# A fused attention and feed-forward kernel: the two weights of an f loaded by one transfer and converted together in operations of 128x768

## The chip, the cores and the metric

One core of a Trainium2 chip. The metric is the device time in microseconds from the start to the end of the kernel. TensorE (PE in the profile, its weight loads PEld) multiplies matrices; the vector engine (DVE) and the scalar engine (ACT) work elementwise; GpSimd (POOL) has only a few fills here; SyncE (SP) issues most of the DMAs, some are issued by ACT.

## The reference

```python
def _attn_ref(q, k, v, beta):                       # each [4, 8, 768, 48], beta [4, 8, 768]
    k_n = k / (np.linalg.norm(k, axis=-1, keepdims=True) + 1e-06)
    for t in range(S):
        kt, vt, bt = (k_n[:, :, t], v[:, :, t], beta[:, :, t, None])
        y[:, :, t] = np.einsum('bhd,bhde->bhe', q[:, :, t], state)
        v_old = np.einsum('bhde,bhd->bhe', state, kt)
        state = state + bt[:, :, :, None] * np.einsum('bhd,bhe->bhde', kt, vt - v_old)
    return y

def _moe_ref(x, w_in, w_out):                       # x [3072, 384], w_in [384, 2048], w_out [2048, 384]
    h = x @ w_in
    g = np.maximum(0.01 * h, h)
    return g @ w_out
```

The output of the first, with its heads laid side by side, is the x of the second.

## The kernel before, in words

The sequence is cut into 12 blocks of 64 steps (`nblk`); a block holds these steps of all four sequences, 256 tokens. Five streams of work run over the blocks. `gram(n)` multiplies keys and queries of a block with its keys (tiles `kq`, `pg`, copied to `gs`) and sends the products through DRAM (`gd`) into the matrix `L`. `inv(b)` inverts the triangular matrix of a block on the vector engine, in 31 elimination steps of short operations on tiles `tmp` and `T` (L263, L268); blocks 0 and 1 are inverted together in the first round, each later block in a round of its own, which begins with a memset of `T` (L280). `solve(n)` carries the recurrent state through the block on TensorE and leaves y in `ys`. `columns(n)` transposes y into x (`px`) and splits it into a high and a low half, `xh` and `xl` (L116). `ffn(n)` is the second part of the reference: for each of 16 pieces f of the hidden width (128 columns each) nine matrix products into `ph` (L468), the activation on ACT (`gh`), the low half `gl` on DVE (L475), and six products into `po` (L458), which follow two f later. At its end two copies `ob` and four output transfers.

All matrix products of the feed-forward part work on pairs of a high and a low part. The weights come from DRAM as 64-bit words, two 32-bit words for each weight (`wr`, 128x384 weights of w_in or of w_out for an f, 384 KB), and `weights()` makes both parts of them once, in block 0. For a piece k (f = k // 2; even k is w_in, odd k w_out) it is: Abs on ACT (L146), a clamp (L148, TENSOR_SCALAR), shift and mask (L154, TENSOR_SCALAR), sign (L155, SCALAR_TENSOR_TENSOR) on `cg`; the rest of the mantissa `cr` (L156, TENSOR_SCALAR, and L157, SCALAR_TENSOR_TENSOR); the exponent `ce` (L158, TENSOR_SCALAR); the cast of `cg` to the high part of `w` on ACT (L160); the low part of `w` on DVE (L161, SCALAR_TENSOR_TENSOR). Raw words and finished weights share a place in memory: the high part is written over the raw words, so the cast waits for L157, which reads them last. There are three `cg` buffers, one `cr` and one `ce`.

What sets the order: the main loop's `weave` calls the streams in turn, in block 0 the conversion over the first 12 of 17 slots; `behind(name)` tells the scheduler not to place an instruction ahead of a marked one. From that a scheduler of the framework fixes the order on each engine. Four pieces (`KA`) are converted ahead of the first inverse, 14 (`WEARLY`) are loaded early, and each later one is loaded eight pieces ahead (`WAHEAD`): the transfer of piece k + 8 waits for a small memset of its tile (L123), which is placed behind the clamp of piece k. Transfers of the weights are issued on SP.

Of the kernel before, what the change touches and what calls it, by code (L numbers as in the profile page):

```python
# [9 lines left out]
F32 = mybir.dt.float32  # L10
F32R = mybir.dt.float32r
U32 = mybir.dt.uint32
U64 = mybir.dt.uint64
AF = mybir.ActivationFunctionType
ALU = mybir.AluOpType
# [16 lines left out]
P = 128  # L32
# [15 lines left out]
def delta_moe_kernel(ctx: ExitStack, tc, kqT, kv, qT, beta, cst, w_all, out, nblk):  # L48
# [10 lines left out]
    nc = tc.nc  # L59
    NFC, _, DO = w_all.shape[1:]  # L60
    NCC = DO // P
    NTB = TB // P

    st = ctx.enter_context(tc.tile_pool(name="st", bufs=1))
    sb = ctx.enter_context(tc.tile_pool(name="sb", bufs=2))
# [34 lines left out]
    def identities():  # L100
        for t in ring["k"]:
            nc.vector.tensor_copy(
                t[0:R0].rearrange("p h u t -> p (h u) t"),
                eye[0:R0, 0:D].rearrange("p (o t) -> p o t", o=1).broadcast_to([R0, GH, D]))


    wi, wo = ([{}, {}] for _ in range(2))
    raws, mark = {}, {}

    def behind(name):  # L110

        return tc.issue_after(mark[name]) if name in mark else nullcontext()
# [2 lines left out]
        nc.scalar.copy(hi, src)  # L115
        nc.vector.tensor_tensor(lo, src, hi.bitcast(F32), ALU.subtract)  # L116

    def load_w(k, gate=None):
        if k < 2 * NFC:
            raws[k] = raw = sb.tile([P, DO], U64, tag=f"w{k}", name=f"wr{k}", bufs=1)  # L120
            if gate:
                with behind(gate):
                    nc.vector.memset(raw[:, 0:1].bitcast(F32), 0.0)  # L123
            with behind("L"):
                nc.sync.dma_start(raw, w_all[:, k // 2, k % 2])

    def weights():

        for k in range(2 * NFC):
            f, x = k // 2, k % 2
            words = raws.pop(k).bitcast(F32).rearrange("p (n two) -> p two n", two=2)
            lo, hi = words[:, 0], words[:, 1]
            loi, hii = lo.bitcast(U32), hi.bitcast(U32)
            g = sb.tile([P, DO], F32, tag="cg", name=f"cg{k}", bufs=CB)
            r = sb.tile([P, DO], F32, tag="cr", name=f"cr{k}", bufs=1)
            gi, ri = g.bitcast(U32), r.bitcast(U32)

            def final():  # L140
                t = sb.tile([P, 2 * DO], F32R, tag=f"w{k}", name=f"w{k}", bufs=1)
                for e in range(2):
                    (wi, wo)[x][e][f] = t[:, e * DO:(e + 1) * DO]
                return (w[f] for w in (wi, wo)[x])

            nc.scalar.activation(g, hi, AF.Abs)  # L146
            with behind("inverse" if k >= KA else None):
                i = nc.vector.tensor_scalar(g, g, HI_MIN, HI_MAX, ALU.max, ALU.min)  # L148
            mark["work"] = i.ins
            if k + WAHEAD >= WEARLY:  # L150
                load_w(k + WAHEAD, "work")

            e = sb.tile([P, DO], F32, tag="ce", name=f"ce{k}", bufs=1)
            nc.vector.tensor_scalar(gi, gi, 3, 0x3FFFF000, ALU.logical_shift_left, ALU.bitwise_and)  # L154
            nc.vector.scalar_tensor_tensor(gi, hii, 0xC0000000, gi, ALU.bitwise_and, ALU.bitwise_or)  # L155
            nc.vector.tensor_scalar(ri, hii, 0x1FF, 14, ALU.bitwise_and, ALU.logical_shift_left)  # L156
            nc.vector.scalar_tensor_tensor(ri, loi, 18, ri, ALU.logical_shift_right, ALU.bitwise_or)  # L157
            nc.vector.tensor_scalar(e.bitcast(U32), gi, 0xFF800000, None, ALU.bitwise_and)  # L158
            d0, d1 = final()
            nc.scalar.copy(d0, g)  # L160
            nc.vector.scalar_tensor_tensor(d1, ri, 2.0 ** -34, e, ALU.mult, ALU.mult)  # L161
            yield

    Lh, gm, nrm, Tts, ys, xs, done = {}, {}, {}, {}, {}, {}, set()
# [1 line left out]
    def need(gen, fn, n):  # L166
        while (fn, n) not in done:
            next(gen)
# [266 lines left out]
    def columns(n):  # L435

        need(sv, solve, n)
        xs[n] = parts = []
        px = [ps_a.tile([P, 2, TB], F32, tag="a", name=f"px{n}_{i}") for i in range(2)]
        for cc in range(NCC):  # L440
            x = px[cc // 2][:, cc % 2]
            for g in range(NGR):
                nc.tensor.matmul(x[:, g * P:(g + 1) * P], ys[n, g][:, cc * P:(cc + 1) * P], eye, start=True, stop=True)
            xh, xl = (sb.tile([P, TB], F32R, tag=t, name=f"{t}{n}_{cc}", bufs=4) for t in ("xh", "xl"))
            split(x, xh, xl)
            parts.append((xh, xl))

    def ffn(n):
        need(sv, solve, n)
        x = xs.pop(n)  # L450
        po = [ps_o.tile([P, 512], F32, tag=f"o{t}", name=f"po{n}_{t}") for t in range(NTB)]
        pend = []

        def second(f, gh, gl):
            for t in range(NTB):
                ts_ = slice(t * P, (t + 1) * P)
                for k, (a, w) in enumerate(((gh, wo[0]), (gh, wo[1]), (gl, wo[0]))):
                    i = nc.tensor.matmul(  # L458
                        po[t][:, :DO], a[:, ts_], w[f],
                        start=(f == 0 and k == 0), stop=(f == NFC - 1 and k == 2))  # L460
            mark["po"] = i.ins

        for f in range(NFC):
            ph = hbank[f % 2][:, f // 2 % 2]
            k = 0
            for cc in range(NCC):
                for a, e in ((wi[0], 0), (wi[0], 1), (wi[1], 0)):
                    nc.tensor.matmul(ph, a[f][:, cc * P:(cc + 1) * P], x[cc][e], start=(k == 0), stop=(k == 3 * NCC - 1))  # L468
                    k += 1
            gh = sb.tile([P, TB], F32R, tag="gh", name=f"gh{n}_{f}", bufs=FB)  # L470
            gl = sb.tile([P, TB], F32R, tag="gl", name=f"gl{n}_{f}", bufs=FB)
            nc.scalar.activation(gh, ph, AF.Prelu, alpha=0.01)  # L472
            i = nc.scalar.activation(ph, ph, AF.Prelu, alpha=0.01)  # L473
            mark["h"] = i.ins
            i = nc.vector.tensor_tensor(gl, ph, gh.bitcast(F32), ALU.subtract)  # L475
            mark["gl"] = i.ins
            pend.append((f, gh, gl))
            if len(pend) > PD:
                second(*pend.pop(0))
            yield  # L480
        if n + 1 < nblk:
            columns(n + 1)
        for a in pend:
            second(*a)
        for t in range(NTB):
            ob = sb.tile([P, DO], F32, tag="cg", name=f"ob{n}_{t}", bufs=CB)
            nc.scalar.copy(ob, po[t][:, :DO])
            for a in range(0, P, C):
                r0 = (t * P + a) // C * nblk * C + n * C
                nc.sync.dma_start(out[r0:r0 + C], ob[a:a + C])  # L490
        yield


    def chain(fn, blocks):
        for n in blocks:
            yield from fn(n)

    def weave(n_slots, *streams):

        taken = [0] * len(streams)  # L500
        for i in range(n_slots):
            for k, (gen, steps, a, b) in enumerate(streams):
                want = steps if i >= b - 1 else max(0, i + 1 - a) * steps // (b - a)
                while taken[k] < want:
                    next(gen, None)
                    taken[k] += 1

    NS, NF, NI = NSLOT, NFC + 1, HC + 1
    wg = weights()
    gg = chain(gram, range(nblk))  # L510
    iv = chain(inv, range(len(NB)))
    sv = chain(solve, range(nblk))
    ff = chain(ffn, range(nblk))
    statics()
    weave(2, (gg, NGR, 0, 2))
    for k in range(KA):
        load_w(k)
    weave(2, (gg, NGR, 0, 2))
    weave(1, (wg, KA, 0, 1))
    identities()  # L520
    weave(1, (iv, NI, 0, 1))
    weave(1, (sv, NS, 0, 1))
    for k in range(KA, WEARLY):
        load_w(k)
    for n in range(nblk):

        weave(NF, (ff, NF, 0, NF), (wg, 2 * NFC * (n == 0), 0, 12), (sv, NS * (n + 1 < nblk), 2, 11),
              (iv, NI * (n + 2 < nblk), 2, NF), (gg, NGR * (n + 3 < nblk), 11, 13))


WAHEAD, WEARLY = 8, 14
KA = 4
CB = 3
PD, FB = 2, 3


# [61 lines left out]
```

## Time and profile before

| | us |
|---|---|
| median of three runs | 724.42 |
| the three runs | 723.74, 724.42, 728.68 |
| the profiled execution, its own time | 727.48 |
| its span from the first to the last instruction | 725.7 |
| PE busy in it | 627.9 |
| DVE busy | 499.6 |
| ACT busy | 323.8 |
| mean granted clock of TensorE | 0.973 |

Busy times are sums over the whole span and mix stages with different limits; the windows view cuts the span into stretches and shows each engine in each of them. A timeline row gives start, duration, engine, line and operation, and in brackets the idle time of the engine ahead of it with what ended it. On DVE a row's duration reaches past the start of the next row, so what an operation takes of the engine in a dense stretch is the distance from start to start. A group row gives count, busy time, mean duration in ns, and the idle time ahead of its instructions with what released them.

### The profile page before, as it was taken

How to read it: one execution, taken by the hardware profiler on the slowest of the kernel's cores; microseconds unless marked ns; L12 is line 12 of the kernel's file. 1: busy time of each engine (PE TensorE's matmuls, PEld its weight loads, DVE VectorE, ACT ScalarE, POOL GpSimd, SP SyncE). 2: the span in 40 equal slices, each digit the busy share in tenths (PEclk: the TensorE clock that was granted, in tenths of full speed). 3: DMA queues.
4: the chain of work that ended last, by engine and by line, in shares of the span. 5: the costliest groups of instructions: out<-in, count | busy, mean ns of one | idle time of the engine just before them, and what ended most of it. 6: DMA issues, size and time to landing. Idle time of an engine off the chain costs nothing.

```text
span 725.7 us, 20966 instructions
## 1 busy us (share of the span) xinstructions
PE 627.9 (87%) x8296; PEld 581.4 (80%) x8296; DVE 499.6 (69%) x2222; ACT 323.8 (45%) x830; POOL 7.4 (1%) x12
## 2 busy tenths in 40 slices
PE   5200789948997999999999999999999999999996
PEld 4100679838986998998989989989989989999996
DVE  7798999999594765866955956947858659532221
ACT  3112656624444463553454444534634635544432
POOL 4000000000000000000000000000000000000000
PEclk9999999967998999999999999999999999999999
DMA  8495783610306427036045064073171260310000
GB/s 196 94 308 106 196 213 91 162 37 23 46 2 121 102 46 162 17 68 153 3 90 131 4 117 105 7 139 77 30 146 48 46 132 2 63 29 2 1 22 23
DMA packets 130786, 60.91 MB, mean 84 GB/s; under 512 B 115392, under 2 KB 118592, under 8 KB 130688
## 3 DMA queue, kind: packets, MB, share of 16 engines
q1 hardware_dynamic: 117376, 56.81, 34.9%
q10 hardware_dynamic: 13312, 2.76, 2.1%
q8 instruction: 65, 1.06, 0.6%
q14 instruction: 33, 0.27, 0.1%
HBM read 46.96 MB, written 12.58 MB: 82 GB/s over the span
## 4 chain that ended last, share of the span: by engine, by line
PE 61%; DVE 22%; DMA 7%; ACT 4%; issue 3%; SPq 2%; ACTq 1%; DVEq 0%
PE ph L468 25%; PE po L458 22%; DMA tt<-T 3%; PE pk L383 3%; DVE rq L216 3%; PE pw L396 3%; DVE rv L388 3%; DVE T L268 2%; DVE tmp L263 2%; PE pu L342 2%; PE pz L334 2%; SPq L307 2%; DVE cg L155 1%; DVE w L161 1%; DVE cr L157 1%
## 5 line engine op out<-in xcount | busy, mean ns | idle before, releaser
L468 PE MATMUL ph<-xh,w 128*128 128x256 f32 x1152 | 257.3, 296 | 10.0 <-DVE gl L475 6.9
L468 PEld LDWEIGHTS ph<-xh,w 128*128 128x128 f32 x1152 | 195.9, 193 | 21.5 <-DVE gl L475 9.7
L458 PE MATMUL po<-w,gh 128*128 128x384 f32 x768 | 192.0, 347 | 8.7 <-ACT w L160 4.9
L475 DVE TENSOR_TENSOR gl<-ph,gh 128x256 fp32r<-128x256 f32 x192 | 80.6, 423 | 134.4 <-ACT ph L473 123.6
L468 PE MATMUL ph<-xl,w 128*128 128x256 f32 x576 | 166.0, 289 | 1.9 <-DVE xl L116 1.1
L472 ACT ACTIVATE gh<-ph 128x256 fp32r<-128x256 f32 x192 | 73.5, 383 | 173.2 <-PE ph L468 170.8
L458 PEld LDWEIGHTS po<-w,gh 128*128 128x128 f32 x768 | 134.1, 193 | 12.1 <-ACT w L160 5.6
L458 PE MATMUL po<-w,gl 128*128 128x384 f32 x384 | 119.7, 345 | 0.0
L468 PEld LDWEIGHTS ph<-xl,w 128*128 128x128 f32 x576 | 111.3, 193 | 4.3 <-DVE xl L116 4.0
L268 DVE TENSOR_TENSOR T<-T,tmp 128x60 f32<-128x60 f32 (+35 forms) x661 | 112.3, 207 | 1.3
L263 DVE TENSOR_TENSOR tmp<-T,L 128x60 f32<-128x60 f32 (+35 forms) x661 | 112.4, 208 | 0.7
L473 ACT ACTIVATE ph<-ph 128x256 f32<-128x256 f32 x192 | 73.1, 381 | 0.0
L458 PEld LDWEIGHTS po<-w,gl 128*128 128x128 f32 x384 | 68.9, 193 | 0.5
L334 PE MATMUL pz<-rt,gm 32*32 32x32 f32 x768 | 19.9, 197 | 34.8 <-DMA rt<-td 34.8
L201 PE MATMUL pg<-kq 48*64 48x128 f32 x768 | 38.5, 301 | 12.5 <-DMA kq<-in_kqT 7.2
L334 PEld LDWEIGHTS pz<-rt,gm 32*32 32x32 f32 x768 | 16.0, 111 | 37.7 <-DMA rt<-td 35.2
L201 PEld LDWEIGHTS pg<-kq 48*64 48x64 f32 x768 | 30.6, 147 | 19.4 <-DMA kq<-in_kqT 8.0
L216 DVE TENSOR_TENSOR rq<-pg,csb 64x256 f32<-64x256 f32 x96 | 40.6, 423 | 1.7
L280 DVE MEMSET T<- 128x512 f32 (+1 forms) x11 | 5.8, 524 | 39.7 <-DMA tt<-T 30.2
L385 ACT ACTIVATE rt<-pk 48x512 f32<-48x512 f32 x44 | 26.1, 593 | 12.6 <-PE pk L383 11.9
L160 ACT CAST w<-cg 128x384 fp32r<-128x384 f32 x32 | 16.1, 510 | 33.6 <-DVE cr L157 24.5
L398 ACT COPY rv<-pw 64x384 f32<-64x384 f32 x48 | 22.7, 472 | 16.1 <-PE pw L396 15.2
(61 smaller groups left out, 651.4 us busy)
## 6 DMA issues: line engine op xcount, KB each, us to landing
wr<-in_w_all SPq DMA_DIRECT2D x32, 384.0 KB, 5.3
kq<-in_kqT SPq DMA_DIRECT2D x44, 192.0 KB, 3.7
L<-gd SPq DMA_DIRECT2D x22, 256.0 KB, 3.9
rk<-in_kv SPq DMA_DIRECT2D x24, 192.0 KB, 3.4
rv<-in_kv SPq DMA_DIRECT2D x24, 192.0 KB, 4.1
rq<-in_qT SPq DMA_DIRECT2D x24, 192.0 KB, 3.8
out<-ob SPq DMA_DIRECT2D x48, 96.0 KB, 2.7
gd<-gs SPq DMA_DIRECT2D x88, 32.0 KB, 2.8
```

The lines of the kernel that those rows point to most:

```text
L201: nc.tensor.matmul(ps[b][c * 64:(c + 1) * 64, p * 128:(p + 1) * 128], kq[r, c ^ b, p, 0], kq[r, c ^ b, p].rearrange("p x t -> p (x t)"), s ...
L216: nc.vector.tensor_tensor(qa[DN, c, b * NPAIR:(b + 1) * NPAIR], pv[b][r, 1], tri[r].rearrange("p (o t) -> p o t", o=1).broadcast_to([C, NP ...
L263: nc.vector.tensor_tensor(tv, t[:, :, j:j + 1].broadcast_to([P, k, w]), L[:, j, j + 1:].rearrange("p (o w) -> p o w", o=1).broadcast_to([P ...
L268: i = nc.vector.tensor_tensor(t, t, tv, ALU.subtract)
L334: nc.tensor.matmul(zv[h * 64:h * 64 + HC, u], gt[lo, l], t[lo, h, u, HC:], start=True, stop=True)
L385: nc.scalar.mul(t[UP, c], pv[c * 64:c * 64 + D], -1.0)
L398: nc.scalar.copy(v[DN, c], pv[c * 64:c * 64 + C])
L458: i = nc.tensor.matmul(po[t][:, :DO], a[:, ts_], w[f], start=(f == 0 and k == 0), stop=(f == NFC - 1 and k == 2))
L468: nc.tensor.matmul(ph, a[f][:, cc * P:(cc + 1) * P], x[cc][e], start=(k == 0), stop=(k == 3 * NCC - 1))
L472: nc.scalar.activation(gh, ph, AF.Prelu, alpha=0.01)
L473: i = nc.scalar.activation(ph, ph, AF.Prelu, alpha=0.01)
L475: i = nc.vector.tensor_tensor(gl, ph, gh.bitcast(F32), ALU.subtract)
```

## The change

`weights()` makes a step for each f rather than for each piece. One transfer brings both weights of an f (768 KB), and every operation of the conversion works on 128x768. The constants follow: two f ahead of the inverse, seven loaded early, four f ahead later on, and two `cg` buffers of 768 columns. The two output copies of a block now fill one such buffer. Line numbers of the new kernel are 7 less below `weights()`, and the operations are L138 (Abs), L140, L145 to L149 and L154 on DVE and L153 (the cast).

```diff
@@ -115,50 +115,43 @@
         nc.scalar.copy(hi, src)
         nc.vector.tensor_tensor(lo, src, hi.bitcast(F32), ALU.subtract)
 
-    def load_w(k, gate=None):
-        if k < 2 * NFC:
-            raws[k] = raw = sb.tile([P, DO], U64, tag=f"w{k}", name=f"wr{k}", bufs=1)
+    def load_w(f, gate=None):
+        if f < NFC:
+            raws[f] = raw = sb.tile([P, 2 * DO], U64, tag=f"w{f}", name=f"wr{f}", bufs=1)
             if gate:
                 with behind(gate):
                     nc.vector.memset(raw[:, 0:1].bitcast(F32), 0.0)
             with behind("L"):
-                nc.sync.dma_start(raw, w_all[:, k // 2, k % 2])
+                nc.sync.dma_start(raw, w_all[:, f].rearrange("p x n -> p (x n)"))
 
     def weights():
 
 
 
-        for k in range(2 * NFC):
-            f, x = k // 2, k % 2
-            words = raws.pop(k).bitcast(F32).rearrange("p (n two) -> p two n", two=2)
+        for f in range(NFC):
+            words = raws.pop(f).bitcast(F32).rearrange("p (n two) -> p two n", two=2)
             lo, hi = words[:, 0], words[:, 1]
             loi, hii = lo.bitcast(U32), hi.bitcast(U32)
-            g = sb.tile([P, DO], F32, tag="cg", name=f"cg{k}", bufs=CB)
-            r = sb.tile([P, DO], F32, tag="cr", name=f"cr{k}", bufs=1)
+            g, r, e = (sb.tile([P, 2 * DO], F32, tag=x, name=f"{x}{f}", bufs=n)
+                       for x, n in (("cg", CB), ("cr", 1), ("ce", 1)))
             gi, ri = g.bitcast(U32), r.bitcast(U32)
-
-            def final():
-                t = sb.tile([P, 2 * DO], F32R, tag=f"w{k}", name=f"w{k}", bufs=1)
-                for e in range(2):
-                    (wi, wo)[x][e][f] = t[:, e * DO:(e + 1) * DO]
-                return (w[f] for w in (wi, wo)[x])
-
             nc.scalar.activation(g, hi, AF.Abs)
-            with behind("inverse" if k >= KA else None):
+            with behind("inverse" if f >= KA else None):
                 i = nc.vector.tensor_scalar(g, g, HI_MIN, HI_MAX, ALU.max, ALU.min)
             mark["work"] = i.ins
-            if k + WAHEAD >= WEARLY:
-                load_w(k + WAHEAD, "work")
-
-            e = sb.tile([P, DO], F32, tag="ce", name=f"ce{k}", bufs=1)
+            if f + WAHEAD >= WEARLY:
+                load_w(f + WAHEAD, "work")
+
             nc.vector.tensor_scalar(gi, gi, 3, 0x3FFFF000, ALU.logical_shift_left, ALU.bitwise_and)
             nc.vector.scalar_tensor_tensor(gi, hii, 0xC0000000, gi, ALU.bitwise_and, ALU.bitwise_or)
             nc.vector.tensor_scalar(ri, hii, 0x1FF, 14, ALU.bitwise_and, ALU.logical_shift_left)
             nc.vector.scalar_tensor_tensor(ri, loi, 18, ri, ALU.logical_shift_right, ALU.bitwise_or)
             nc.vector.tensor_scalar(e.bitcast(U32), gi, 0xFF800000, None, ALU.bitwise_and)
-            d0, d1 = final()
-            nc.scalar.copy(d0, g)
-            nc.vector.scalar_tensor_tensor(d1, ri, 2.0 ** -34, e, ALU.mult, ALU.mult)
+            t = sb.tile([P, 2, 2 * DO], F32R, tag=f"w{f}", name=f"w{f}", bufs=1)
+            for k in range(2):
+                wi[k][f], wo[k][f] = t[:, k, :DO], t[:, k, DO:]
+            nc.scalar.copy(t[:, 0], g)
+            nc.vector.scalar_tensor_tensor(t[:, 1], ri, 2.0 ** -34, e, ALU.mult, ALU.mult)
             yield
 
     Lh, gm, nrm, Tts, ys, xs, done = {}, {}, {}, {}, {}, {}, set()
@@ -483,7 +476,9 @@
         for a in pend:
             second(*a)
         for t in range(NTB):
-            ob = sb.tile([P, DO], F32, tag="cg", name=f"ob{n}_{t}", bufs=CB)
+            if t == 0:
+                obs = sb.tile([P, NTB, DO], F32, tag="cg", name=f"ob{n}", bufs=CB)
+            ob = obs[:, t]
             nc.scalar.copy(ob, po[t][:, :DO])
             for a in range(0, P, C):
                 r0 = (t * P + a) // C * nblk * C + n * C
@@ -524,13 +519,13 @@
         load_w(k)
     for n in range(nblk):
 
-        weave(NF, (ff, NF, 0, NF), (wg, 2 * NFC * (n == 0), 0, 12), (sv, NS * (n + 1 < nblk), 2, 11),
+        weave(NF, (ff, NF, 0, NF), (wg, NFC * (n == 0), 0, 12), (sv, NS * (n + 1 < nblk), 2, 11),
               (iv, NI * (n + 2 < nblk), 2, NF), (gg, NGR * (n + 3 < nblk), 11, 13))
 
 
-WAHEAD, WEARLY = 8, 14
-KA = 4
-CB = 3
+WAHEAD, WEARLY = 4, 7
+KA = 2
+CB = 2
 PD, FB = 2, 3
```

The vector engine in the dense part of the conversion, between two rounds of the inverse; a number behind a name is that of the buffer's use. Before:

```order
L148 TENSOR_SCALAR cg_1067<-cg_1067 128x384
L123 MEMSET wr_1071 128x2
L157 SCALAR_TENSOR_TENSOR cr_917<-wr_768,cr_917 128x384
L154 TENSOR_SCALAR cg_1067<-cg_1067 128x384
L161 SCALAR_TENSOR_TENSOR w_929<-cr_917,ce_923 128x384
L155 SCALAR_TENSOR_TENSOR cg_1067<-wr_772,cg_1067 128x384
L156 TENSOR_SCALAR cr_933<-wr_770 128x384
L158 TENSOR_SCALAR ce_939<-cg_932 128x384
```

The same place in the changed kernel:

```order
L140 TENSOR_SCALAR cg_1150<-cg_1150 128x768
L123 MEMSET wr_1155 128x2
L149 TENSOR_SCALAR ce_1104<-cg_1102 128x768
L148 SCALAR_TENSOR_TENSOR cr_1103<-wr_784,cr_1103 128x768
L145 TENSOR_SCALAR cg_1150<-cg_1150 128x768
L154 SCALAR_TENSOR_TENSOR w_1115<-cr_1103,ce_1104 128x768
L146 SCALAR_TENSOR_TENSOR cg_1150<-wr_820,cg_1150 128x768
L147 TENSOR_SCALAR cr_1151<-wr_820 128x768
L140 TENSOR_SCALAR cg_1166<-cg_1166 128x768
```

The same seven operations stand there for an f rather than for a piece, and the clamp of the next `cg` (`cg_1166`, which takes the place of `cg_1102`) stands five rows behind the last read of the raw words of the f before (L148).

The scalar engine ahead of the first inverse, around the last writes of `gd`. Before:

```order
L209 DMA gd_185<-gs_0_186 32x8x32 x2
L205 COPY gs_1_218<-pg_1_0_220 128x256
L160 CAST w_287<-cg_277 128x384
L205 COPY gs_1_218<-pg_1_1_221 128x256
L160 CAST w_300<-cg_290 128x384
L209 DMA gd_185<-gs_1_218 32x8x32 x2
```

Of the changed kernel:

```order
L202 DMA gd_181<-gs_0_182 32x8x32 x2
L198 COPY gs_1_214<-pg_1_0_216 128x256
L153 CAST w_270<-cg_260 128x768
L198 COPY gs_1_214<-pg_1_1_217 128x256
L202 DMA gd_181<-gs_1_214 32x8x32 x2
```

One cast less stands ahead of the last transfer of `gd`.

The vector engine between the first and the second `xl` of block 0, whose three stand at the start of its feed-forward part. Before:

```order
L116 TENSOR_TENSOR xl_0_703<-px_0_698,xh_0_702 128x256
L161 SCALAR_TENSOR_TENSOR w_1096<-cr_1084,ce_1090 128x384
L155 SCALAR_TENSOR_TENSOR cg_1235<-wr_852,cg_1235 128x384
L156 TENSOR_SCALAR cr_1220<-wr_836 128x384
L158 TENSOR_SCALAR ce_1226<-cg_1219 128x384
L148 TENSOR_SCALAR cg_1251<-cg_1251 128x384
L123 MEMSET wr_1255 128x2
L157 SCALAR_TENSOR_TENSOR cr_1220<-wr_836,cr_1220 128x384
L154 TENSOR_SCALAR cg_1251<-cg_1251 128x384
L116 TENSOR_TENSOR xl_1_709<-px_0_698,xh_1_708 128x256
```

Of the changed kernel:

```order
L116 TENSOR_TENSOR xl_0_673<-px_0_668,xh_0_672 128x256
L149 TENSOR_SCALAR ce_1152<-cg_1150 128x768
L148 SCALAR_TENSOR_TENSOR cr_1151<-wr_820,cr_1151 128x768
L145 TENSOR_SCALAR cg_1166<-cg_1166 128x768
L154 SCALAR_TENSOR_TENSOR w_1163<-cr_1151,ce_1152 128x768
L146 SCALAR_TENSOR_TENSOR cg_1166<-wr_836,cg_1166 128x768
L147 TENSOR_SCALAR cr_1167<-wr_836 128x768
L140 TENSOR_SCALAR cg_1214<-cg_1214 128x768
L123 MEMSET wr_1219 128x2
L149 TENSOR_SCALAR ce_1168<-cg_1166 128x768
L148 SCALAR_TENSOR_TENSOR cr_1167<-wr_836,cr_1167 128x768
L116 TENSOR_TENSOR xl_1_679<-px_0_668,xh_1_678 128x256
```

Seven operations of 384 columns and a small memset stood between the two; now it is nine of 768 and a memset.

## Rows read from the trace of the kernel before

**Rows 1.** Windows, core 0: stretch, length, PE, PEld, DVE, ACT, POOL, PEclk, DMA, GB/s
```profile
0.00:69.00 69.00, 13.55 (x130) 11.48 (x130) 58.91 (x220) 12.38 (x24) 7.35 (x12) 1.00 0.71 178
69.00:140.00 71.00, 60.52 (x996) 54.35 (x1000) 66.85 (x220) 44.90 (x108) 0.00 (x0) 0.95 0.67 164
140.00:173.00 33.00, 20.84 (x114) 17.46 (x107) 32.48 (x117) 11.17 (x27) 0.00 (x0) 0.69 0.20 45
173.00:233.00 60.00, 54.55 (x710) 49.88 (x708) 41.94 (x233) 27.03 (x68) 0.00 (x0) 0.96 0.29 49
233.00:642.00 409.00, 400.24 (x5552) 372.12 (x5553) 282.18 (x1396) 195.90 (x514) 0.00 (x0) 0.99 0.36 76
```

**Rows 2.** Waits of PE, 140 to 173 us: us in total, times, longest
```profile
PE po L458 <- ACT w L160: 4.9, 3, 2.5
PE ph L468 <- ACT w L160: 2.7, 4, 0.9
```

**Rows 3.** Groups by form, all engines: count, busy us, mean ns, idle before
```profile
L157 DVE SCALAR_TENSOR_TENSOR cr<-wr,cr 128x384 uint32<-128x384 uint32 x32 | 17.7, 552 | 0.2
...
L146 ACT ACTIVATE cg<-wr 128x384 f32<-128x384 f32 x32 | 17.5, 553 | 8.6 <-DMA wr<-in_w_all 6.7 <-issue 1.2 <-DVE ce L158 0.2
...
L205 ACT COPY gs<-pg 128x256 f32<-128x256 f32 x48 | 15.9, 375 | 29.8 <-PE pg L201 29.8
...
L292 DVE TENSOR_TENSOR L<-L,cb 128x512 f32<-128x512 f32 x22 | 14.2, 688 | 0.1
...
L416 ACT COPY ys<-py 128x384 f32<-128x384 f32 x24 | 11.5, 478 | 2.4 <-PE py L414 1.9
...
L148 DVE TENSOR_SCALAR cg<-cg 128x384 f32<-128x384 f32 x32 | 11.2, 352 | 1.7 <-ACT cg L146 1.6
...
L102 DVE COPY rk<-csb 64x768 f32<-64x768 f32 x2 | 2.6, 1328 | 0.3 <-DMA csb<-in_cst 0.3
...
L245 DVE TENSOR_SCALAR sr<-sr 128x32 f32<-128x32 f32 x11 | 2.0, 181 | 0.3
```

**Rows 4.** Timeline of DVE, 87.2 to 90 us: start, length, engine, line
```profile
87.29 0.55 DVE L161 SCALAR_TENSOR_TENSOR w<-cr,ce 128x384 fp32r<-128x384 uint32 x1
87.76 0.55 DVE L155 SCALAR_TENSOR_TENSOR cg<-wr,cg 128x384 uint32<-128x384 uint32 x1
88.22 0.35 DVE L156 TENSOR_SCALAR cr<-wr 128x384 uint32<-128x384 uint32 x1
88.49 0.35 DVE L158 TENSOR_SCALAR ce<-cg 128x384 uint32<-128x384 uint32 x1
...
89.78 0.55 DVE L161 SCALAR_TENSOR_TENSOR w<-cr,ce 128x384 fp32r<-128x384 uint32 x1
```

**Rows 5.** Timeline of DVE, ends of the stage from 68 to 173 us
```profile
68.83 0.48 DVE L280 MEMSET T<- 128x512 f32 x1 [1.15 <-DMA td<-T]
...
72.35 0.36 DVE L148 TENSOR_SCALAR cg<-cg 128x384 f32<-128x384 f32 x1 [1.64 <-ACT cg L146]
...
172.86 0.42 DVE L116 TENSOR_TENSOR xl<-px,xh 128x256 fp32r<-128x256 f32 x1
```

**Rows 6.** Timeline of ACT, and of DVE at 33.55 us, before the inverse
```profile
8.75 0.56 ACT L146 ACTIVATE cg<-wr 128x384 f32<-128x384 f32 x1 [2.27 <-DMA wr<-in_w_all]
9.77 0.55 ACT L146 ACTIVATE cg<-wr 128x384 f32<-128x384 f32 x1 [0.46 <-DMA wr<-in_w_all]
...
27.34 0.51 ACT L160 CAST w<-cg 128x384 fp32r<-128x384 f32 x1 [1.38 <-DVE cr L157]
27.34 0.81 ACTq L209 DMA_DIRECT2D gd<-gs  x2
...
33.55 0.19 DVE L239 TENSOR_SCALAR sr<-L 128x32 uint32<-128x32 uint32 x1 [4.17 <-DMA L<-gd]
```

**Rows 7.** Windows of PE alone: stretch, length, busy, PEclk, DMA, GB/s
```profile
140.00:150.00 10.00, 4.97 (x57) 1.00 0.61 135
150.00:160.00 10.00, 6.04 (x19) 0.50 0.06 13
```

## The prediction

> **What bounds the kernel now.** I read the windows view first, cut where TensorE's share changes [rows 1]. Until 69 us the vector engine is busy 58.91 of 69 us and TensorE 13.55. From 69 to 173 us it stays that way: the vector engine has 66.85 + 32.48 = 99.3 us of work in 104 us, TensorE 60.52 + 20.84 = 81.4. From 233 us on it is the other way round, TensorE 400.24 of 409 us. The blocks between 173 and 233 us have both below full. So a shorter conversion of the weights can move the time only by bringing forward the moment at which the vector engine is through with it. What comes behind is TensorE's and moves along as a whole.
>
> Then the waits of TensorE in the last of that stage [rows 2]: the two largest groups, 4.9 and 2.7 us, are waits for weights, 7.6 us together. They end when a cast of the conversion (L160) ends, which itself follows the vector engine. The vector engine's own timeline has no gap to speak of there: the T memset at 68.83 us opens the stage after 1.15 us of idling, one wait of 1.64 us for the Abs follows at 72.35, and at 172.86 the xl is made which opens the next block's first matrix product [rows 5]. Between these two marks lie 104.0 us; this is the stretch that the change shortens.
>
> **The change part by part.** *Fewer, wider operations on the vector engine.* Before, each of 32 pieces is seven operations, four TENSOR_SCALAR (352 ns) and three SCALAR_TENSOR_TENSOR (552 ns) [rows 3]. But they overlap at their ends: in the stage, one starts 0.27 us after a TENSOR_SCALAR and 0.46 to 0.47 after a SCALAR_TENSOR_TENSOR, and from one L161 to the next it is 89.78 - 87.29 = 2.49 us [rows 4]. The pair of an f so takes 4.98 us. What the second 384 columns cost I take from slopes: a TENSOR_SCALAR of 32 columns takes 181 ns, one of 384 columns 352, so 171/352 = 0.486 ns a column, 0.187 us for 384; a TENSOR_TENSOR of 512 columns takes 688 and a SCALAR_TENSOR_TENSOR of 384 takes 552, 136/128 = 1.06 ns a column, 0.408 us for 384 [rows 3]. A wide set then takes 2.49 + 4 x 0.187 + 3 x 0.408 = 4.46 us, 0.52 less than two narrow sets. Two f are converted before the inverse in both kernels, so 14 f lie on the path of the vector engine: 14 x 0.52 = 7.3 us.
>
> No operation of 128x768 stands in this trace, so the bounds. Low: each of the seven removed operations gives back all that isn't columns, 352 - 187 = 165 ns and 552 - 408 = 144 ns, 4 x 0.165 + 3 x 0.144 = 1.09 us an f, 15.3 in all. High: the one operation with 768 columns in the trace is a copy of 64x768 at 1328 ns [rows 3], far above the 0.54 that the slope gives a TENSOR_SCALAR. At 1.33 us for each of seven an f would take 9.3 us, 4.3 more than now, and the kernel 60 more. That copy ran in the first stage, the only one where the GpSimd is busy, 7.35 us against 0.00 later [rows 1], and it reads one matrix over and over, so I set it aside. In between: a wide set that costs two narrow ones, no gain. I take 7.3, from the rows of the same operations.
>
> The overlap of 0.08 us between one operation and the next is what decides between 7.3 and 15.3. [...]
>
> *Scalar engine.* Abs (553 ns) and cast (0.51 us) go from four an f to two; by 375 ns at 256 columns and 478 at 384, 0.80 ns a column, they become 0.86 and 0.82 us, 1.68 an f in place of 2.13. It is busy 44.90 of 71 us, so nothing is gained there [rows 1, 3, 6]; what hides it is the vector engine.
>
> *The ring of cg, two wide buffers in place of three narrow.* The Abs of f+1 waits for the cast of f-1, and the cast waits for the operation that reads the raw words last (the cr of L157, now L148), since it writes over them. In the new order four operations stand between that one and the clamp of the next cg: 0.46 + 0.87 + 0.87 + 0.46 = 2.66 us, against 0.82 + 0.86 = 1.68 for cast and Abs. There is 0.98 us of cover; I cost it at nothing. If the cover is gone, what is queued behind the waiting clamp is the whole vector engine, elimination of the inverse included, and TensorE waits behind that.
>
> *The start.* One transfer of 768 KB in place of two: the first Abs starts at 8.75 us and the second at 9.77, each on its data, so the first f can now begin when its second half is there, 1.0 us later. Against this the last write of gd was issued at 27.34 us, when a cast went that had waited 1.38 us for the vector engine. That second cast is gone from there, so L can land up to 1.4 us earlier than 33.55, where the vector engine had stood for 4.17 us. The weights loaded within the inverse come whole in the same way, and operations of 0.9 in place of 0.5 us lie between the short steps of the elimination [rows 6]. I take 0 for all of it, with 2 us to both sides.
>
> *The order.* The xl of block 0's second and third columns now stand behind larger operations, some 3 us later in the order, and with them the FFN of block 0. It has weights ready by then that it had to wait for before; I take 0. *The output copies:* the four transfers of a block start behind both copies. In the steady blocks nothing waits for them; at the very end at most a copy's 0.48 us [rows 3] is at stake; 0.
>
> Sum: -7.3 us. Against the profiled execution's own time, 727.48 us (725.7 of span and 1.8 outside), that is 720.2. The median of the three runs is 724.42, 3.1 below the profiled one, and the same 7.3 us taken off gives 717.1.
>
> **The rivals.** *A: the fixed cost goes as a whole.* For it: the slopes do show 144 to 165 ns an operation. Against it: the overlap in rows 4. Then 15.3 us are gained: 709.1. [...]
>
> *B, the slower side: the ring of cg makes the vector engine wait for the scalar engine in each f.* For it: the clamp waited 1.64 us for an Abs once already, and the scalar engine, busy 63% there, may have other work ahead of cast and Abs. Against it: over 32 clamps the idle time before L148 was 1.7 us in all, 1.6 of it that one [rows 3, 5]. The cover is 0.98 us and the gain 0.52, so it decides from a delay of 1.5 us an f. Four instructions of some 0.478 us ahead of cast and Abs make 1.9 us: the wait is 0.92, times 14 is 12.9, less 7.3 is 5.6 us slower: 730.0.
>
> *C: TensorE becomes the bound in block 0.* [...] Its FFN starts later, and it has 81.4 us of work in what would be 97. If 8 more us of its matmuls at full clock fall into a half-clock stretch, they take 16, and, with the gaps that it has while it waits for attention, some 4 of these 8 us show at the end: 7.3 - 4 = 3.3, or 721.1. Against it: 7.6 us of its waits are for weights, and they shrink first.
>
> *D: the change does not do what it says,* wide operations cost as much as two: 724.4.
>
> **How the numbers follow.** Forecast 0.52, A 0.13, B 0.11, C 0.20, D 0.04. One per cent, 7.2 us, is about what a measurement of this kernel can tell from no change, and my forecast lies on that bound, at 717.2. Of its 0.52, 0.31 fall below (the removed operations can hardly give less than the slopes say, and may give some more) and 0.21 above. Faster: 0.31 + 0.13 and 0.02 of C = 0.46; same: 0.21 + 0.18 + 0.04 = 0.43; slower: 0.11. The range goes from A's time, with little over, to 2 us above no change: 708.5 to 726.5. It leaves out most of B and some of what lies beyond A.
>
> **What would show it.** In the new profile the wide TENSOR_SCALAR should take some 0.54 us and the wide SCALAR_TENSOR_TENSOR 0.96; from one L154 to the next in the dense stage 4.4 to 4.5 us. From the first T memset behind the inverse to the last xl of block 1 there should be about 97 us. Idle time before L140, released by the Abs, should stay under 2 us in all; more of it would be B. TensorE's waits for weights in block 0's last third should shrink from 7.6 us to a few. Blocks from 233 us on should keep their length. I am wrong if the stage is shorter by over 11 us or under 4, or if the first memset comes more than 2 us off 68.83.

## The result and the profile after

The changed kernel took 717.83 us (median of 4 runs, 715.63 to 720.66) against 726.55 us for the kernel before in the same comparison (723.74 to 729.53): a ratio of 0.9885, 95% interval 0.9856 to 0.9914, or 8.4 us less. It was measured twice more beside the experiments: 0.9907 (0.9875 to 0.9939) and 0.9900 (0.9872 to 0.9927). The forecast, 7.3 us off, was a ratio of 0.990.

The profiled execution of the changed kernel took 720.66 us, the slowest of its four, with a span of 718.9. Its windows, cut at its own marks, answer to [rows 1] (columns as there):

```profile
0.00:70.00 70.00, 14.05 (x130) 11.61 (x130) 59.86 (x200) 12.61 (x20) 7.35 (x12) 1.00 0.71 182
70.00:140.00 70.00, 59.15 (x804) 53.03 (x805) 67.26 (x135) 40.37 (x79) 0.00 (x0) 0.90 0.53 141
140.00:164.00 24.00, 21.92 (x302) 20.10 (x301) 23.44 (x101) 10.82 (x30) 0.00 (x0) 1.00 0.55 118
164.00:222.00 58.00, 52.46 (x709) 48.00 (x707) 41.73 (x235) 27.10 (x68) 0.00 (x0) 1.00 0.30 52
222.00:635.00 413.00, 400.87 (x5550) 372.34 (x5551) 281.26 (x1395) 195.87 (x514) 0.00 (x0) 0.99 0.36 75
```

The picture is the same as before: the vector engine is full until 164 us (67.26 of 70, then 23.44 of 24), TensorE from 222 us on. What has changed is the place of the cut, 164 us where it stood at 173.

The wide operations, in the view of groups by form, answer to [rows 3]:

```profile
L148 DVE SCALAR_TENSOR_TENSOR cr<-wr,cr 128x768 uint32<-128x768 uint32 x16 | 15.2, 952 | 0.1
...
L138 ACT ACTIVATE cg<-wr 128x768 f32<-128x768 f32 x16 | 14.6, 921 | 9.6 <-DMA wr<-in_w_all 9.0 <-DVE ce L149 0.5
...
L153 ACT CAST w<-cg 128x768 fp32r<-128x768 f32 x16 | 13.3, 831 | 20.9 <-DVE cr L148 13.3 <-DMA td<-T 3.0 <-DMA rt<-td 2.5
...
L140 DVE TENSOR_SCALAR cg<-cg 128x768 f32<-128x768 f32 x16 | 8.8, 555 | 1.8 <-ACT cg L138 1.8
```

The clamp takes 555 ns, the SCALAR_TENSOR_TENSOR 952; the slopes gave 0.54 and 0.96. Abs and cast take 921 and 831 ns, where 0.86 and 0.82 us were expected. And so it looks on the vector engine's timeline in the dense part, which answers to [rows 4]:

```profile
87.49 0.95 DVE L154 SCALAR_TENSOR_TENSOR w<-cr,ce 128x768 fp32r<-128x768 uint32 x1
88.36 0.95 DVE L146 SCALAR_TENSOR_TENSOR cg<-wr,cg 128x768 uint32<-128x768 uint32 x1
89.23 0.55 DVE L147 TENSOR_SCALAR cr<-wr 128x768 uint32<-128x768 uint32 x1
89.70 0.55 DVE L140 TENSOR_SCALAR cg<-cg 128x768 f32<-128x768 f32 x1
...
91.52 0.55 DVE L145 TENSOR_SCALAR cg<-cg 128x768 uint32<-128x768 uint32 x1
91.99 0.95 DVE L154 SCALAR_TENSOR_TENSOR w<-cr,ce 128x768 fp32r<-128x768 uint32 x1
```

From L154 to the next L154 are 91.99 - 87.49 = 4.50 us for the seven operations of an f (forecast 4.46), where two pieces took 4.98. Starts lie 0.47 to 0.48 us apart behind a TENSOR_SCALAR and 0.87 behind a SCALAR_TENSOR_TENSOR, so the overlap of 0.08 us at the end of each operation is there as before. In this stretch no operation reads or overwrites what the one just ahead of it uses; two f alternate.

The marks on the same timeline answer to [rows 5] and to the last of [rows 6]; the fifth row is the memset of T for the fourth inverse, which in the kernel before stood at 225.17 us:

```profile
32.58 0.19 DVE L232 TENSOR_SCALAR sr<-L 128x32 uint32<-128x32 uint32 x1 [3.89 <-DMA L<-gd]
...
69.88 0.48 DVE L273 MEMSET T<- 128x512 f32 x1 [0.84 <-DMA td<-T]
...
73.02 0.56 DVE L140 TENSOR_SCALAR cg<-cg 128x768 f32<-128x768 f32 x1 [1.25 <-ACT cg L138]
...
164.25 0.41 DVE L116 TENSOR_TENSOR xl<-px,xh 128x256 fp32r<-128x256 f32 x1
...
213.78 0.48 DVE L273 MEMSET T<- 128x512 f32 x1 [6.45 <-DMA tt<-T]
...
232.08 0.19 DVE L232 TENSOR_SCALAR sr<-L 128x32 uint32<-128x32 uint32 x1 [5.11 <-DMA L<-gd]
```

L lands 1.0 us earlier (33.55 before), the first memset behind the inverse comes 1.05 us later (68.83), the last xl of block 1 8.6 us earlier (172.86) and the memset for the fourth inverse 11.4 us earlier. The last row, a wait of 5.11 us for L, has no counterpart at this place before. TensorE's waits of [rows 2] for weights have gone: the largest wait from 140 to 173 us is now another one (columns as in [rows 2]),

```profile
PE po L451 <- DVE gl L468: 1.3, 1, 1.3
```

and there is no row with w among them.

**The vector engine's time, counted.** For the comparisons below I count, up to the memset of T for the fourth inverse, how long the vector engine was occupied: the moment of that memset less all idle times in brackets on its timeline until then. Before that is 225.17 - 28.67 = 196.5 us, after 213.78 - 25.76 = 188.0 us: 8.5 us less. Of the 11.4 us won at that point the other 2.9 are idle time that fell. In the two other profiles of the changed kernel the occupied time is 188.0 and 187.8 us, the memset comes at 215.64 and 213.46 and the idle time is 27.6 and 25.7: the first number repeats, the idle time less so.

### The profile page after: what moved, and what is told of

The parts are those of the page before. It is cut to its first block, busy times and chain, and to the rows that moved or that the text cites. A ratio compares the mean times of both kernels' runs of the same rounds, so it can differ in the third digit from the quotient of the medians.

```text
span 718.9 us, 20764 instructions
## 1 busy us (share of the span) xinstructions
PE 626.8 (87%) x8296; PEld 581.4 (81%) x8296; DVE 491.0 (68%) x2101; ACT 319.2 (44%) x798; POOL 7.3 (1%) x12
## 4 chain that ended last, share of the span: by engine, by line
PE 61%; DVE 17%; DMA 10%; SPq 4%; ACT 4%; issue 2%; ACTq 1%; DVEq 0%
PE ph L461 25%; PE po L451 22%; DMA tt<-T 3%; PE pk L376 3%; PE pw L389 3%; DVE T L261 3%; DVE tmp L256 3%; DVE rv L381 2%; DVE rq L209 2%; PE pu L335 2%; DMA wr<-in_w_all 2%; SPq L300 2%; PE pz L327 1%; PE px L436 1%; DMA gd<-gs 1%
## 5 line engine op out<-in xcount | busy, mean ns | idle before, releaser
L451 PE MATMUL po<-w,gh 128*128 128x384 f32 x768 | 188.9, 343 | 2.7 <-ACT gh L465 2.7
L198 ACT COPY gs<-pg 128x256 f32<-128x256 f32 x48 | 15.9, 375 | 33.4 <-PE pg L194 31.6
```

What stands on the lines that cost most here:

```text
L451: i = nc.tensor.matmul(po[t][:, :DO], a[:, ts_], w[f], start=(f == 0 and k == 0), stop=(f == NFC - 1 and k == 2))
```

## The experiments

Unless another is named, each edit is to the changed kernel. Ratios are to the kernel before, measured beside it on the same chip.

### Width of the operations, and number of transfers

Narrow operations in the changed frame: each of the seven split into two halves, shown for one of them.

```diff
-            nc.vector.tensor_scalar(ri, hii, 0x1FF, 14, ALU.bitwise_and, ALU.logical_shift_left)
+            hs = [slice(x * DO, (x + 1) * DO) for x in range(2)]
+            for h in hs:
+                nc.vector.tensor_scalar(ri[:, h], hii[:, h], 0x1FF, 14, ALU.bitwise_and, ALU.logical_shift_left)
```

> The changed kernel with each of its seven conversion operations on the vector engine split into two of 128x384 (transfer, Abs, cast and order constants stay those of the change). If the gain is the width of the operations (0.065 to 0.07 us of start-to-start time for each of 98 operations that went), one f takes about 4.98 us again in the dense stage, where the changed kernel shows 4.50, and the time goes back by about 7 us: ratio to before 0.996 to 1.003. If it is the single transfer, the order or the output copies, the ratio stays at 0.989.

Measured: 1.0008 (0.9984 to 1.0033). The gain is gone. The pairs stand in its timeline as "x2", two halves in one row:

```profile
87.62 0.63 DVE L152 TENSOR_SCALAR cr<-wr 128x384 uint32<-128x384 uint32 x2
88.17 0.62 DVE L156 TENSOR_SCALAR ce<-cg 128x384 uint32<-128x384 uint32 x2
88.70 1.02 DVE L154 SCALAR_TENSOR_TENSOR cr<-wr,cr 128x384 uint32<-128x384 uint32 x2
89.64 0.62 DVE L141 TENSOR_SCALAR cg<-cg 128x384 f32<-128x384 f32 x2
```

A pair of narrow TENSOR_SCALAR takes 0.53 to 0.55 us from start to start and a pair of SCALAR_TENSOR_TENSOR 0.94, against 0.47 and 0.87 in one piece. The vector engine was occupied 195.8 us up to the fourth inverse, 7.8 more than with wide operations and 0.7 less than before.

Two transfers of 384 KB, wide operations:

```diff
-                nc.sync.dma_start(raw, w_all[:, f].rearrange("p x n -> p (x n)"))
+                for x in range(2):
+                    nc.sync.dma_start(raw[:, x * DO:(x + 1) * DO], w_all[:, f, x])
```

> The changed kernel with two transfers of 384 KB for an f in place of one of 768 KB, operations 768 wide. If the gain is the width of the operations, the ratio to before stays at 0.985 to 0.993 and one f takes 4.50 us in the dense stage. If the single transfer brought it, the ratio is 0.996 to 1.003.

Measured: 0.9948 (0.9921 to 0.9975), between the two expectations. So it was measured again, with the changed kernel itself beside it:

> The changed kernel a third time, beside the two next, for a narrower comparison: ratio to before 0.988 to 0.992.

> Two loads of 384 KB an f with wide operations, again. If only the vector engine's time counted, it is within 0.002 of the changed kernel in the same call (its vector engine was occupied for 188.9 us up to the fourth inverse, against 188.0). If the waits that its order of instructions makes in the blocks 0 and 1 count as well, it stays 0.003 to 0.006 above.

Measured: 0.9900 (0.9872 to 0.9927) for the changed kernel, 0.9944 (0.9920 to 0.9968) for two transfers. The four corners:

| | narrow operations | wide operations |
|---|---|---|
| two transfers an f | 1 (the kernel before) | 0.9948, 0.9944 |
| one transfer an f | 1.0008 | 0.9885, 0.9907, 0.9900 |

The first corner is not an exact one: the kernel before also has 32 narrow Abs and casts, three narrow `cg` buffers and its own output copies. In the run with narrow operations these are as in the changed kernel, so one transfer together with all of them brings nothing. Width with two transfers brings half a per cent, both together one. The vector engine's occupied time is almost that of the changed kernel in both profiles with two transfers (188.9 and 188.7 us), so width does there what it does here. The remaining 3 us or so are thus not occupied time of the vector engine. The memset for the fourth inverse came at 219.26 and 216.42 us with an idle time of 30.3 and 27.8 us; but the changed kernel's second profile had 27.6 us of idle time there too, and its span was 715.2 us against 718.1 in the second of these, so the idle time alone does not account for them. The second transfer also changes the order that the scheduler makes: the last xl of block 1 comes earlier than in the changed kernel (161.68 and 160.43 us against 164.25), the fourth inverse later. Whether it is the transfer or this order was not settled.

### The price of a microsecond on the vector engine

The exponent made twice (the second result is the same as the first):

```diff
             nc.vector.tensor_scalar(e.bitcast(U32), gi, 0xFF800000, None, ALU.bitwise_and)
+            nc.vector.tensor_scalar(e.bitcast(U32), gi, 0xFF800000, None, ALU.bitwise_and)
```

> The changed kernel with the operation for the exponent (a TENSOR_SCALAR of 128x768, 0.475 us from start to start) made twice for each f. That adds 16 x 0.475 = 7.6 us to the vector engine. If the engine's time up to the memset of T for the fourth inverse sets the end one for one, the kernel is 5 to 8 us slower than the changed one: ratio to before 0.996 to 1.000. If the vector engine has slack there, or what is won or lost ahead of that memset is evened out behind it by the wait for L, it costs under 3 us: 0.989 to 0.993.

> The changed kernel itself, once more, beside the others: every theory expects a ratio to before of 0.986 to 0.992, as measured first (0.9885). It is there because two loads an f in place of one gave 0.9948, which should not differ from this one if only the width of the operations mattered.

Measured: 1.0002 (0.9976 to 1.0027) with the extra operation, 0.9907 for the changed kernel beside it, a difference of 0.0095 or 6.9 us. The two groups in its profile,

```profile
L150 DVE TENSOR_SCALAR ce<-cg 128x768 uint32<-128x768 uint32 x16 | 8.9, 553 | 0.2
L149 DVE TENSOR_SCALAR ce<-cg 128x768 uint32<-128x768 uint32 x16 | 8.8, 551 | 0.0
```

are 16 operations each. Occupied time rose by 7.4 us (195.4), and the kernel's time by 6.9. So the vector engine's occupied time up to the fourth inverse passes almost one for one into the kernel's time here. The moment of that memset does not: the next run shows it.

### The ring of cg

```diff
-CB = 2
+CB = 1
```

> The changed kernel with one cg buffer in place of two. The Abs of the next f then waits for the cast of this one, which waits for L148: 0.83 + 0.92 = 1.75 us from the end of L148 to the next clamp, of which the low part L154 covers 0.87. If the ring is what the vector engine runs close to, it now waits up to 0.9 us an f, 14 times: up to 12 us more than the changed kernel, ratio to before 0.997 to 1.006, less where the elimination steps fill the gap. If a ring of two had cover to spare and the scheduler fills the rest with other work, the ratio stays below 0.993.

Measured: 0.9938 (0.9913 to 0.9964), some 3 us above the changed kernel, and near the lower of the two. The wait of which the expectation speaks does not stand where it was looked for:

```profile
L140 DVE TENSOR_SCALAR cg<-cg 128x768 f32<-128x768 f32 x16 | 8.9, 554 | 0.5 <-ACT cg L138 0.4
```

In all 16 clamps it is 0.5 us. The order of the instructions, made for one buffer, puts other work ahead of the clamp. The cost came as occupied time, 192.3 us, 4.3 more with the same number of instructions. Counted from start to start, less bracketed idle time, the conversion's seven operations and the small memsets take 79.3 us in place of 74.9, which is all of it, and the timeline shows where:

```profile
89.94 0.95 DVE L146 SCALAR_TENSOR_TENSOR cg<-wr,cg 128x768 uint32<-128x768 uint32 x1
90.93 0.56 DVE L149 TENSOR_SCALAR ce<-cg 128x768 uint32<-128x768 uint32 x1
91.52 0.96 DVE L154 SCALAR_TENSOR_TENSOR w<-cr,ce 128x768 fp32r<-128x768 uint32 x1
92.52 0.56 DVE L147 TENSOR_SCALAR cr<-wr 128x768 uint32<-128x768 uint32 x1
```

Here each operation reads what the one ahead has just written (ce of cg, w of ce) or overwrites what it reads (cr), and it starts 0.99, 0.59 and 1.00 us after that one, where 0.87 and 0.47 lie between operations that have nothing to do with each other. The overlap of 0.08 us is gone, and 0.03 to 0.04 us of pause has taken its place. So the overlap comes from the order in which two f alternate, which the second `cg` buffer allows.

The memset for the fourth inverse came at 222.20 us, 8.4 behind the changed kernel's first profile, and the kernel took only some 3 us more: in this profile the vector engine did not wait for L behind it. With two buffers the clamp's waits for the Abs were 1.8 us in all, 1.25 of it at 73.02 us (the group of L140 and the timeline's row in the section on the result). A ring of two had cover.

### The clamp on GpSimd

```diff
-                i = nc.vector.tensor_scalar(g, g, HI_MIN, HI_MAX, ALU.max, ALU.min)
+                i = nc.gpsimd.tensor_scalar(g, g, HI_MIN, HI_MAX, ALU.max, ALU.min)
```

> The changed kernel with the clamp (L140) of each f on GpSimd, which is idle from 69 us on. It takes 14 x 0.475 = 6.7 us from the vector engine's path. If GpSimd takes under 3 us for one and does not slow the vector engine, the time falls by 3 to 6 us: ratio to before 0.980 to 0.986. If the clamp is much slower there (over 4 us, so that the conversion waits for it), or the two engines slow each other, the time is that of before or above: 0.995 to 1.010.

Measured: 1.0515 (1.0479 to 1.0550), far above both expectations. In the groups of GpSimd,

```profile
L140 POOL TENSOR_SCALAR cg<-cg 128x768 f32<-128x768 f32 x16 | 66.4, 4161 | 55.3 <-ACT cg L138 55.3
```

one clamp takes 4.16 us on average, 7.5 times what the vector engine takes, and on the vector engine's timeline the next step waits for it:

```profile
57.21 0.94 DVE L148 SCALAR_TENSOR_TENSOR cr<-wr,cr 128x768 uint32<-128x768 uint32 x1
...
60.99 1.17 DVE L145 TENSOR_SCALAR cg<-cg 128x768 uint32<-128x768 uint32 x1 [2.66 <-POOL cg L140]
```

The L145 behind the wait also took 1.17 us where the changed kernel shows 0.55, while GpSimd was at its next clamp (two of them stand in one row, from 54.45 to 63.69 us). These waits are 18.4 us in all, less than half of what the run lost. The order is another one as well: all 16 f are converted ahead of the first memset behind the inverse, four in the changed kernel, and that memset came at 145.26 us in place of 69.88; from 70 to 145 us TensorE was busy 0.00 us. So the ratio is that of a slow clamp and of this order together.

### The wait for L

In the changed kernel's profile SP issues this around the wait of 5.11 us (timeline of SP; L177, L359 and L360 load kq, rv and rq, L202 writes gd, L217 reads L):

```profile
217.52 0.99 SPq L177 DMA_DIRECT2D kq<-in_kqT  x2
218.62 1.88 SPq L202 DMA_DIRECT2D gd<-gs  x4
220.54 0.48 SPq L359 DMA_DIRECT2D rv<-in_kv  x1
221.07 0.58 SPq L360 DMA_DIRECT2D rq<-in_qT  x1
221.75 0.37 SPq L177 DMA_DIRECT2D kq<-in_kqT  x1
222.26 1.87 SPq L202 DMA_DIRECT2D gd<-gs  x4
224.17 0.45 SPq L177 DMA_DIRECT2D kq<-in_kqT  x1
224.66 0.47 SPq L359 DMA_DIRECT2D rv<-in_kv  x1
227.20 1.10 SPq L217 DMA_DIRECT2D L<-gd  x2
```

L is issued 5.7 us behind the last xl of block 2 (221.51 us); before it was 1.0 us (233.94 behind 232.90). Two loads of kq for the sixth block stand ahead of the eight writes of gd for the fifth, rv, rq and a third kq among them, a fourth kq and an rv behind them. L needs all writes of gd, and SP stood 1.9 us until they had landed: these took 3.6 us from issue to landing (median) where before they took 2.3. The vector engine stands until 232.08, gl behind it, and TensorE's timeline shows the wait for that gl:

```profile
234.07 0.38 PE L461 MATMUL ph<-xh,w 128*128 128x256 f32 x1 [2.13 <-DVE gl L468]
```

Its windows around it (columns as in [rows 7]):

```profile
232.00:236.00 4.00, 1.93 (x21) 0.85 0.28 75
236.00:240.00 4.00, 4.00 (x72) 0.50 0.04 8
240.00:244.00 4.00, 4.00 (x49) 0.80 0.00 0
```

It was busy 1.93 of 4 us at a granted clock of 0.85 on average, and then was granted 0.50 for the next four. Matrix products of 128x256 that follow one another start 0.21 us apart there, and 0.12 us from 242 us on, where it was granted 1.00 again. The first attempt set the mark "L", behind which all loads of the recurrence and of the keys are placed, anew for each block from the fifth on:

```diff
-                if n == 1:
+                if n == 1 or n >= 4:
                     mark["L"] = d.ins
```

> The changed kernel with the loads of the recurrence and of the keys placed behind the load of L for blocks from the fifth on as well. [...] If that gives back part of the gain, the wait of 5.11 us goes, and the time falls by 2 to 4 us against the changed kernel: ratio to before 0.983 to 0.987. If TensorE's work bounds there anyway, the ratio stays at 0.988 to 0.990.

Measured: 1.0559 (1.0507 to 1.0610). The loads were now too late in every block; the vector engine's waits from 216 to 400 us show it:

```profile
DVE rv L381 <- DMA rv<-in_kv: 24.3, 7, 5.4
```

So only the loads of kq for the sixth block were held back:

```diff
                 if n == 1:
                     mark["L"] = d.ins
+                if n == 4:
+                    mark["L4"] = d.ins
...
-            with behind("L"):
+            with behind("L4" if n == 5 else "L"):
                 for b in range(2):
```

> The changed kernel with only the loads of kq for the sixth block held behind the load of L for the fifth; the loads of the recurrence keep their places, which the last attempt moved as well (the vector engine then waited for rv in every block, 24.3 us in the trace from 216 to 400 us). If the wait of 5.11 us for L gives back part of the gain, L now comes some 2 to 4 us earlier behind the last xl of block 2 and the time falls by 1 to 4 us against the changed kernel: ratio 0.983 to 0.988. If TensorE's work bounds there, the ratio is that of the changed kernel, within 0.002.

Measured: 0.9881 (0.9843 to 0.9918), median 714.4 us, against 0.9907 for the changed kernel: too close to tell. So it was measured again:

> The loads of kq for the sixth block behind L, again. If the wait for L gave back part of the gain it is 0.002 to 0.005 below the changed kernel in the same call; if not, within 0.002 of it.

Measured: 0.9841 (0.9816 to 0.9867), median 714.3 us, against 0.9900 (0.9872 to 0.9927); the intervals don't overlap. SP's timeline of that run:

```profile
217.63 2.01 SPq L202 DMA_DIRECT2D gd<-gs  x4
219.68 0.45 SPq L362 DMA_DIRECT2D rq<-in_qT  x1
220.22 0.47 SPq L361 DMA_DIRECT2D rv<-in_kv  x1
220.74 0.58 SPq L362 DMA_DIRECT2D rq<-in_qT  x1
221.42 1.87 SPq L202 DMA_DIRECT2D gd<-gs  x4
225.45 1.10 SPq L217 DMA_DIRECT2D L<-gd  x2
226.65 2.47 SPq L487 DMA_DIRECT2D out<-ob  x4
229.16 2.86 SPq L177 DMA_DIRECT2D kq<-in_kqT  x4
```

L is issued at 225.45 us, 4.5 us behind the last xl of block 2 (220.93) in place of 5.7, with the kq behind it. And the same hold in the kernel before:

> The kernel before with the same hold as the last one: the loads of kq for the sixth block behind the load of L for the fifth. In the trace of before L is issued 1.0 us behind the last xl of block 2 and the vector engine does not wait for it. If the hold only takes away a wait that came with the change, the ratio to before is 0.997 to 1.003. If it helps either kernel, it is 0.992 to 0.996.

Measured: 0.9980 (0.9954 to 1.0007). No gain can be told from nothing there, though the interval reaches to almost half a per cent. So this version beats both kernels, and most of what it takes away seems to have come with the change. That it works through the wait for L is not shown: in its two profiles the wait was 0.93 and 3.66 us, against 5.11, 3.68 and 4.91 in the three of the changed kernel, and the hold moved other instructions too: both loads of rq stand among the writes of gd in its timeline, while the changed kernel issues the second at 231.34 us, behind L.

## Why the prediction was right

*What bounds the kernel* held in the main. Occupied time given to the vector engine ahead of the fourth inverse came out at the end (7.4 us cost 6.9, and the narrow operations' 7.8 took the whole gain back).

*The price of a wide operation* held: 4.50 us for an f against 4.46, so 0.48 less than two narrow sets where 0.52 was forecast. The choice between 7.3 and 15.3 us was made by the overlap, start-to-start times rather than durations, and that is what the trace shows: a removed operation gives back 0.065 us (2 x 0.27 - 0.475 for a TENSOR_SCALAR, 2 x 0.467 - 0.87 for a SCALAR_TENSOR_TENSOR), not the 0.144 to 0.165 us of its duration that are not columns. Rival A would have been 15.3 us and falls, and D, no gain from the width, falls by the narrow operations, 1.0008. The overlap is no property of the operations alone: with one `cg` buffer it was gone wherever an operation depends on the one just ahead. Where none does, it is 0.08 us in the wide form as in the narrow (wide 0.95 less 0.87 and 0.55 less 0.47, narrow 0.55 less 0.47 and 0.35 less 0.27).

*The count of 14 f* was too small: the two f converted ahead of the inverse save theirs too. The occupied time fell by 8.5 us. Sixteen f at the dense stretch's 0.48 us are 7.7 of it. Counted on the two timelines from start to start, the seven operations and the small memsets take 83.6 us before and 74.9 after, which is the whole fall. What is over the 7.7 comes from stretches where they do not stand packed and from nine memsets fewer, a term that the sum did not have; how it divides was not separated. *The start* came out at +1.05 us at the first memset, inside the 2 us that were left to both sides: L landed 1.0 us earlier, and from there to the memset it took 37.3 us in place of 35.3. By then the changed kernel had finished four f where the one before had finished three, which I had not counted.

*The stage* was shorter than forecast: 94.4 us from the first memset to the last xl of block 1 in place of 97. A part of the 9.7 us that it lost is that fourth f (4.5 us), which moved ahead of the mark.

*"What comes behind is TensorE's and moves along as a whole"* held only in part, and it is the weak step of the prediction. At the fourth inverse the three profiles of the changed kernel are 11.4, 9.5 and 11.7 us ahead of the one of before, at the end of the span 6.8, 10.5 and 9.2. In all three the lead first shrinks, from the last xl of block 2 to the last xl of block 4, by 4.9, 0.9 and 4.9 us, and grows again by 0.3 to 2.4 behind it. In the first and the third profile TensorE's granted clock fell around the wait for L (on average 0.74 and 0.77 from 230 to 240 us), in the second it was 1.00 there; with the hold on the four loads the lead shrinks by 1.1 and 0.9. These are single executions, and those of the kernel before alone spread from 721.43 to 729.53 us; what is clear of noise is that a hold on four loads brought 2 to 4 us more. SP's order had changed with the vector engine's, and loads had moved ahead of the L of the fifth block; I had looked at the order on the vector engine, ScalarE and TensorE for this, not on SP.

So the total came out close in part by luck: the vector engine's occupied time fell by more than the sum had (8.5 us for 7.3), idle time ahead of the fourth inverse fell by 1.1 to 3.0, which the sum did not have either, and in two of three profiles part of both was lost behind it.

*Rivals B and C* did not come: the clamp waited 1.8 us in all; TensorE waited for no weights behind 140 us. TensorE's clock averaged 0.90 from 70 to 140 us and 1.00 from there to 222, where before it was 0.95 from 69 to 140 and 0.69 from 140 to 173 us: the time at 0.50 lay earlier and was shorter (an estimate from these means, which takes the rest as granted 1.00: 14 us of the 70, against 7 and 20), while the vector engine still set the pace. That 8 us of matrix products take 16 in a half-clock stretch, such as the second of [rows 7], was an estimate of the prediction; at 0.50 products of 128x256 started 0.21 us apart in the changed kernel, at 1.00 0.12, which is 1.8 times.

## What to carry to other kernels

To price a merge of small operations, take the distance from start to start in a dense stretch of the trace, for the short and for the long form (by a slope), and not the duration of one: here that is 65 ns for each operation removed instead of 150, and it holds as long as neighbours do not depend on each other: behind one that they depend on, operations started 0.12 us later. Count all the work ahead of the point where the bound changes, not only that of the stage in view, and give the engine an extra copy of one operation to see whether its time passes through. When instructions get shorter, read the DMA queue's order too: here its order had changed unnoticed, and a hold on four loads was worth 2 to 4 us, by a path that was not shown.

## What was not expected of the hardware

GpSimd took 4.16 us on average for a clamp of 128x768 fp32 that the vector engine does in 0.555, and the vector engine's own TENSOR_SCALAR of the same size beside it took 1.17 us at 60.99 us in place of 0.55 (548 ns on average for L145 in the changed kernel).

A vector operation that reads or overwrites what the one just ahead uses started 0.03 to 0.04 us after that one's end, an independent one 0.08 us before it (the run with one `cg` buffer, and the dense part of the changed kernel).

One wait of 2.1 us on TensorE, in a block which it bounds, was followed by a stretch at half the clock in the changed kernel's first profile (granted 0.50 from 236 to 240 us); in its second profile the same four microseconds were granted 1.00. Such stretches differed here from one execution of the program to the next, so a few microseconds at that place are not settled by one profile.
